# The last 64 outputs of a second matrix product, regrouped: two feed-forward blocks side by side instead of two halves of the tokens

## The chip, the cores and the metric

One core of one Trainium2 chip runs the kernel. The metric is device time in microseconds (us) of one execution, median of three runs. The product runs on TensorE (PE in the rows), the elementwise work on VectorE (DVE) and ScalarE (ACT); SyncE (SP) issues the DMAs. PE has two clock levels, 1.2 and 2.4 GHz; a granted clock of 1.00 is 2.4 GHz.

## The reference

```python
w = softmax(weight_gen, axis=-1)                     # (8, 4096, 8 heads, 7 taps)
x = sum over k of w[..., k] * x_pad[s + k]           # causal convolution, 8 heads of 24 channels
x = x.reshape(32768, 192)
h = x @ w_in                                         # 192 -> 2048
g = np.maximum(h, 0.0) ** 2
out = g @ w_out                                      # 2048 -> 192
```

All inputs and outputs are 32-bit floats.

## The kernel before

The 32768 tokens are worked in 64 chunks of 512. DVE does a chunk's softmax and convolution, the result goes through memory and back to be turned (tokens along the free dimension), and is then split into two 16-bit parts, `xh` on ACT and `xl` on DVE.

The first product (`mm1`, L560) makes the 2048 hidden values of a chunk in eight steps j of two blocks of 128. Three 16-bit products stand in for one 32-bit one, so a step has nine accumulation rounds of 512 columns. Every matmul uses a 64x64 quarter of the array, and four of them run side by side. ACT takes the relu (L567), the square (L571) and a 16-bit copy `gh` (L575); DVE makes the rest `gl` (L579).

The second product (`mm2_turned`, L608 and L612) serves chunks 4 to 62, 59 of them. It has 192 outputs, of which 128 go to the accumulator `acc0`, as two column halves of 64. The last 64 go to `acc1`: one column half of the array takes tokens 0 to 255 of the chunk, the other tokens 256 to 511, with the same weights. The two row halves of the array hold the two halves of a block's 128 hidden values; they write two different halves of the accumulator's free dimension, which have to be added at the end. `n` counts the three 16-bit products, `gh`, `gh` and `gl`.

The order of the work is written out by hand in one loop over chunks `c` and stages `b` = 0 to 3; each engine runs its own part of it in that order. A stage is two steps of `mm1`, then the second product of the stage before it. In stage (c, 1), ahead of the first `mm2` of chunk c, `finish` empties the accumulators of chunk c-1: ACT copies one half out (L674), DVE adds the other (L675). `store_turned` then scales (L697), turns 32x32 blocks (L698) and issues 24 DMAs on SP (L705). All this stands behind the two `low` (L579) of stage (c, 0) in DVE's order. Work of the convolution for later chunks is handed to stages by `plan_conv`, into the table `todo`, which runs at the end of a stage. Odd chunks also load the next group of two chunks at b = 0 (L109, L110), sum its magnitudes on ACT at b = 2 (L137), and make its scales at b = 3 in six short DVE instructions (L141 to L166, L151).

Of the kernel before, what the change touches and what calls it, by code (L numbers as in the profile page):

```python
# [8 lines left out]
F32 = mybir.dt.float32  # L9
# [4 lines left out]
ALU = mybir.AluOpType  # L14
# [14 lines left out]
def kernel(  # L29
# [9 lines left out]
    nc = tc.nc  # L39
    B, S, D = x.shape  # L40
# [3 lines left out]
    P = 128  # L44
# [4 lines left out]
    TC = 4  # L49
    NCH = n_chunks or R // TC  # L50
# [3 lines left out]
    D1 = 64  # L54
    ND = D // D1
    N = TC * P
    NJ = NF // 2
# [3 lines left out]
    N_PE = 3  # L61
# [8 lines left out]
    op = ctx.enter_context(tc.tile_pool(name="op", bufs=2))  # L70
# [13 lines left out]
    V = const.tile([P, NF, 3 * D], F16, name="V")  # L84
# [6 lines left out]
    act, ts, tt = nc.scalar.activation, nc.vector.tensor_scalar, nc.vector.tensor_tensor  # L91
# [100 lines left out]
    def block(j, i):  # L192
        return 4 * (j // 2) + 2 * i + j % 2
# [101 lines left out]
    HALVES = slice(0, D1), slice(D1, P)  # L295
# [240 lines left out]
    phs, rgs, ghs, gls, accs = {}, {}, {}, {}, {}  # L536

    def turned(c):
        return TURNED <= c < NCH - 1
# [33 lines left out]
    def high(c, j):  # L573
        gh = ghs[c, j] = gp.tile([P, 2, N], F16, name="gh")
        act(gh, rgs[c, j], AF.Copy, scale=1.0 / LIFT)  # L575
# [21 lines left out]
    def mm2_turned(c, j):  # L597
        if j == 0:
            new_accs(c)
        gh, gl = ghs.pop((c, j)), gls.pop((c, j))  # L600
        for i in range(2):
            fb = block(j, i)
            for n, g in enumerate((gh, gh, gl)):
                fl = dict(start=fb == 0 and n == 0, stop=fb == NF - 1 and n == 2)
                for col in HALVES:
                    for r, rows in enumerate(HALVES):
                        d = n * D + col.start
                        nc.tensor.matmul(accs[c][0][col, r], V[rows, fb, d:d + D1], g[rows, i], **fl)  # L608
                for m, col in enumerate(HALVES):
                    for r, rows in enumerate(HALVES):  # L610
                        d = n * D + P
                        nc.tensor.matmul(  # L612
                            accs[c][1][col, r, 0:N // 2], V[rows, fb, d:d + D1],
                            g[rows, i, m * N // 2:(m + 1) * N // 2], **fl,
                        )

    ends = {}

# [40 lines left out]
    outs, sums_t = {}, {}  # L659

    def finish(c, p):
        if c == 0:
            if p == 0:
                outs[c] = op.tile([P, TC, D], F32, name="o_sb")
            nc.scalar.copy(outs[c][:, 2 * p:2 * p + 2], accs[c][0][:, :, p * D:(p + 1) * D])
            return
        acc = accs[c][p]
        if turned(c):
            if p == 0:
                sums_t[c] = op.tile([P, TC * D], F32, name="s", bufs=1)  # L670
            n0, n1 = ((0, N), (N, N + N // 2))[p]
            n = n1 - n0
            tmp = op.tile([P, N], F32, name="tmp")
            nc.scalar.copy(tmp[:, 0:n], acc[:, 1, 0:n])  # L674
            tt(out=sums_t[c][:, n0:n1], in0=acc[:, 0, 0:n], in1=tmp[:, 0:n], op=ALU.add)  # L675
            return
        if p == 0:
            outs[c] = op.tile([P, TC, D], F32, name="o_sb")
        o = outs[c][:, 2 * p:2 * p + 2]
        f = falls[c // CPG]  # L680
        o = o.rearrange("p t d -> p (t d)")
        tmp = op.tile([P, N], F32, name="tmp")
        n = 2 * D
        act(tmp[:, 0:n], acc[:, 1, 0:n], AF.Copy, scale=f)
        stt(out=o, in0=acc[:, 0, 0:n], scalar=f, in1=tmp[:, 0:n], op0=ALU.mult, op1=ALU.add)  # L685

    def finish_last(c):
        o = outs[c]
# [4 lines left out]
    def store_turned(c):  # L693
        o = op.tile([P, TC * D], F32, name="o_sb")
        sm = sums_t.pop(c)
        sb = sm.rearrange("p (t n) -> p t n", n=P)
        tt(out=sb, in0=sb, in1=spread_falls[c // CPG].broadcast_to(sb.shape), op=ALU.mult)  # L697
        nc.vector.transpose(o, sm)  # L698
        for col in range(0, D, Q):
            for t in range(TC):  # L700
                if col < P:
                    p0, n0 = col, t * P
                else:
                    p0, n0 = 2 * t // TC * D1 + col - P, N + t % 2 * P
                nc.sync.dma_start(  # L705
                    out=out_v[:, c * TC + t, col:col + Q].rearrange("(q i) j -> i q j", i=Q),
                    in_=o[p0:p0 + Q, n0:n0 + P].rearrange("i (q j) -> i q j", j=Q),
                )

    def store(c):  # L710
        nc.sync.dma_start(out=out_v[:, c * TC:(c + 1) * TC, :], in_=outs[c])
# [128 lines left out]
    def at(c, b, f):  # L840
        todo.setdefault((c + b // NB, b % NB), []).append(f)
# [9 lines left out]
    def plan_conv(m):  # L851
        a, splits[m] = conv_steps(m, int(m < N_PE))
        if m == N_PE:
            for f in a[:6]:
                at(m - 2, 3, f)
            rows = splits.pop(m)
            for i, f in enumerate(a[6:-1]):
                at(m - 1, int(i > 4), f)
            between[m - 1, 1] = [a[-1], rows[0]]
            behind[m - 1, 1] = rows[1:]  # L860
            return
        for f in a[:3]:
            at(m - 2, 2 * int(m == N_PE + 1), f)
        if m > N_PE:
            spread(a[3:], m - 2, 1, pace.get(m, (0.25, 0.55, 0.73, 1)))

    pace = {N_PE + 1: (0, 0, 0.41, 0.7, 1), N_PE + 2: (0, 0.42, 0.72, 1)}
    splits = {}
    for u in range(1, NU):
        at(1, u - 1, cvt[NU + u][0])  # L870
        at(1, u, cvt[NU + u][1])
# [11 lines left out]
    for c in range(1, NCH + 1):  # L883
        for b in range(NB if c < NCH else 2):
            js = (2 * b, 2 * b + 1)
            if c < NCH:
                if b == 0 and c % 2 and (c + 3) // 2 * CPG < NCH:
                    load_group((c + 3) // 2)
                if c % 2 and b == 2 and (c + 3) // 2 * CPG < NCH:
                    total, scales = size_steps((c + 3) // 2)  # L890
                    b1 = 5 if c == 1 else 2
                    at(c, b1, total)
                    b2 = 6 if c == 1 else 3
                    at(c, b2, scales)
                    at(c, b2, lambda gi=(c + 3) // 2: descale(gi))
                if b == 0 and c + 2 < NCH and c + 2 > 2:
                    plan_conv(c + 2)
                for j in js:
                    mm1(c, j)
            early = b == 1 and 2 <= c <= TURNED  # L900
            if early:
                for p in range(2):
                    finish(c - 1, p)
            run(late)
            late.clear()
            if c == NCH and b == 1:
                finish_last(c - 1)
            elif b == (0 if c == NCH else 1) and c > 1:
                for p in range(0 if early else 2):
                    finish(c - 1, p)  # L910
                if turned(c - 1):
                    store_turned(c - 1)
                elif c < NCH:
                    store(c - 1)
            turn = turns.pop(c + 1, None) if b == NB - 1 else None
            if b == NB - 1 and c + 1 in splits and turn is None:
                for f in splits.pop(c + 1):
                    f()
            if pend and turn is None:
                mm2(*pend.pop(0))  # L920
            elif pend:
                one = pend.pop(0)
                mm2(*one, slice(0, 3))
                turn[0]()
                mm2(*one, slice(3, 4))
                turn[1]()
                mm2(*one, slice(4, 8))
            if c < NCH:
                relu(c, js[0])
                square(c, js[0])  # L930
                relu(c, js[1])
                high(c, js[0])
                sp = splits.pop(c + 1) if turn is not None else []
                run(sp[:1])
                square(c, js[1])
                run(sp[1:3])
                high(c, js[1])
                pend.append((c, b))
                late += [lambda c=c, j=js[0]: low(c, j)] + between.pop((c, b), [])
                late += [lambda c=c, j=js[1]: low(c, j)] + behind.pop((c, b), [])  # L940
                fs = todo.pop((c, b), [])
                if sp:
                    run(fs[:2])
                    run(sp[3:4])
                    run(fs[2:4])
                    run(sp[4:])
                    run(fs[4:])
                else:
                    run(fs)
# [30 lines left out]
```

## Time and profile before

| | |
|---|---|
| median of 3 runs | 2035.33 us (2034.96 to 2036.3) |
| the profiled execution | 2034.99 us |
| its span, first to last instruction | 2032.9 us |
| PE busy | 2024.2 us (100%), 42124 matmuls |
| weight loads | 1467.5 us (72%) |
| DVE busy | 1861.3 us (92%) |
| ACT busy | 1746.0 us (86%) |
| granted clock of PE | 1.000 |

Times in the rows are us from the first instruction. "Busy" is the union of an engine's instructions; ends of matmuls are modelled, so starts are what to compare. A row of a timeline gives the start, the time from there to the end of the last of the merged instructions, the engine, the line, the operation, the tiles written and read, the shape and the count; in brackets stands how long the engine was idle before it and who released it. Instructions of one engine overlap a little, so the start of the next one tells what one costs.

### The profile page before, as it was taken

The page shows a single profiled execution, that of the slowest core. Times are in us where ns is not written, and L with a number is a line of the kernel's source. Part 1 is how long each engine was busy: PE and PEld are TensorE (multiplying, and loading weights), DVE is VectorE, ACT ScalarE, POOL GpSimd, SP SyncE. Part 2 cuts the span into 40 slices and gives each one's busy share as a digit, 9 for nine tenths or more (in the row PEclk, how much of TensorE's full clock was granted, in tenths as well). Part 3 has the DMA queues.
Part 4 walks back from the last instruction along what each step waited for, and adds up shares of the span by engine and source line. Part 5 has one row for each costly group of instructions (what it writes and reads, how often), then busy time and mean ns, then how long its engine had stood idle before and what let it go on. Part 6 is the DMA issues. An engine that isn't in the chain of part 4 may idle for free.

```text
span 2032.9 us, 92331 instructions
## 1 busy us (share of the span) xinstructions
PE 2024.2 (100%) x42124; PEld 1467.5 (72%) x42124; DVE 1861.3 (92%) x2457; ACT 1746.0 (86%) x2011; POOL 5.4 (0%) x9
## 2 busy tenths in 40 slices
PE   9999999999999999999999999999999999999999
PEld 7777777777777777777777777777777777777776
DVE  8999999999999999999999999999999999999984
ACT  6888888888888888888888888888888888888887
POOL 1000000000000000000000000000000000000000
PEclk9999999999999999999999999999999999999999
DMA  6233333333332333233323333333233233333221
GB/s 189 67 95 86 79 65 76 89 94 76 69 84 74 96 83 83 62 79 89 93 73 64 91 75 94 84 76 70 73 95 93 72 65 82 82 95 78 59 60 23
DMA packets 303552, 164.02 MB, mean 81 GB/s; under 512 B 215360, under 2 KB 273728, under 8 KB 299192
## 3 DMA queue, kind: packets, MB, share of 16 engines
q1 hardware_dynamic: 303160, 158.11, 31.8%
q8 instruction: 329, 5.39, 1.1%
q14 instruction: 63, 0.52, 0.1%
HBM read 108.43 MB, written 49.56 MB: 78 GB/s over the span
## 4 chain that ended last, share of the span: by engine, by line
PE 95%; DVE 3%; DMA 1%; ACT 0%; SPq 0%; issue 0%; POOL 0%; DVEq 0%; POOLq 0%
PE ph L560 47%; PE acc L608 30%; PE acc L612 15%; PE acc L653 1%; PE acc L592 1%; DVE pr L339 1%; DVE pr L344 1%; DVE gl L579 1%; DMA xT<-xd 0%; DMA xl<-xd 0%; DMA xd<-xr 0%; DVE o_sb L685 0%; PE ph L628 0%; SPq L117 0%; DMA xt<-in_x_dram 0%
## 5 line engine op out<-in xcount | busy, mean ns | idle before, releaser
L560 PEld LDWEIGHTS <-W 64*64 64x64 f16 (+1 forms) x17568 | 633.7, 107 | 320.6 <-issue 4.1
L560 PE MATMUL ph<-xh,W 64*64 64x512 f16 (+1 forms) x11712 | 752.9, 376 | 0.0
L567 ACT ACTIVATE g<-ph 128x1024 f32<-128x1024 f32 x504 | 511.5, 1015 | 240.5 <-PE ph L560 240.5
L579 DVE SCALAR_TENSOR_TENSOR gl<-gh,g 128x1024 f16<-128x1024 f16 x504 | 609.2, 1220 | 110.5 <-ACT gh L575 99.7
L608 PE MATMUL acc<-gh,V 64*64 64x512 f16 x7552 | 696.3, 376 | 0.0
L612 PE MATMUL acc<-gh,V 64*64 64x256 f16 x7552 | 576.9, 269 | 0.1
L608 PEld LDWEIGHTS <-V 64*64 64x64 f16 x11328 | 406.7, 107 | 205.9 <-issue 1.3
L571 ACT ACTIVATE g<-g 128x1024 f32<-128x1024 f32 x512 | 538.7, 1052 | 8.0
L575 ACT ACTIVATE gh<-g 128x1024 f16<-128x1024 f32 x504 | 530.2, 1052 | 8.0
L560 PE MATMUL ph<-xl,W 64*64 64x512 f16 (+1 forms) x5856 | 427.0, 376 | 2.1 <-DMA xl<-xd 1.7
L612 PEld LDWEIGHTS <-V 64*64 64x64 f16 x11328 | 406.6, 107 | 17.3 <-issue 0.4
L339 DVE TENSOR_TENSOR pr<-xt,wt 128x768 f32<-128x768 f32 x434 | 408.2, 953 | 2.1
L608 PE MATMUL acc<-gl,V 64*64 64x512 f16 x3776 | 389.4, 376 | 0.5 <-DVE gl L579 0.5
L344 DVE TENSOR_TENSOR pr<-pr 128x768 f32<-128x768 f32 x376 | 358.4, 953 | 2.2
L612 PE MATMUL acc<-gl,V 64*64 64x256 f16 x3776 | 288.4, 269 | 0.0
L393 DVE TENSOR_TENSOR xl<-xT,xh 128x512 f16<-128x512 f32 x180 | 113.5, 686 | 21.5 <-ACT xh L387 20.8
L387 ACT CAST xh<-xT 128x512 f16<-128x512 f32 x180 | 98.5, 610 | 1.1 <-DMA xT<-xd 1.1
L653 PE MATMUL acc<-V,gh 64*128 64x192 f16 x960 | 62.1, 243 | 0.0
L520 DVE STREAM_TRANSPOSE xr<-pr 128x768 f32<-128x768 f32 x60 | 58.7, 978 | 2.1
L653 PE MATMUL acc<-V,gl 64*128 64x192 f16 x480 | 60.2, 243 | 0.1
L675 DVE TENSOR_TENSOR s<-acc,tmp 128x512 f32<-128x512 f32 x118 | 59.9, 549 | 0.0
L698 DVE STREAM_TRANSPOSE o_sb<-s 128x768 f32<-128x768 f32 x59 | 57.7, 978 | 2.1
(98 smaller groups left out, 661.7 us busy)
## 6 DMA issues: line engine op xcount, KB each, us to landing
xT<-xd SPq DMA_DIRECT2D x120, 384.0 KB
xt<-in_x_dram SPq DMA_DIRECT2D x31, 1344.0 KB
xd<-xr SPq DMA_DIRECT2D x240, 96.0 KB
out_dram<-o_sb SPq DMA_DIRECT2D x1416, 16.0 KB
wt<-in_weight_gen_dram SPq DMA_DIRECT2D x31, 224.0 KB
raw<-in_moe_w_in_dram SPq DMA_DIRECT2D x8, 384.0 KB
raw<-in_moe_w_out_dram SPq DMA_DIRECT2D x4, 768.0 KB
fd<-ft SPq DMA_DIRECT2D x124, 0.1 KB
```

Of the source, the lines that this page charges most:

```text
L339: tt(out=dst, in0=src, in1=taps_w[0][:, :, k:k + 1].broadcast_to([P, n, G]), op=ALU.mult)
L344: on.tensor_tensor(out=prs[k0], in0=prs[k0], in1=prs.pop(k), op=ALU.add)
L387: nc.scalar.copy(xh, xs)
L393: tt(out=xl, in0=xs, in1=xh, op=ALU.subtract)
L560: nc.tensor.matmul(to, w[rows, k, j % 2, col], xs, **fl)
L567: act(r, phs.pop((c, j)), AF.Relu, scale=RHO * LIFT ** 0.5)
L571: act(r, r, AF.Square)
L575: act(gh, rgs[c, j], AF.Copy, scale=1.0 / LIFT)
L579: stt(out=gl, in0=ghs[c, j], scalar=-LIFT, in1=rgs.pop((c, j)), op0=ALU.mult, op1=ALU.add)
L608: nc.tensor.matmul(accs[c][0][col, r], V[rows, fb, d:d + D1], g[rows, i], **fl)
L612: nc.tensor.matmul(accs[c][1][col, r, 0:N // 2], V[rows, fb, d:d + D1], g[rows, i, m * N // 2:(m + 1) * N // 2], **fl,)
L653: nc.tensor.matmul(accs[c][t // 2][:, h, t % 2 * D:(t % 2 + 1) * D], g[rows, i, t * P:(t + 1) * P], V[rows, fb, n * D:(n + 1) * D], start= ...
```

## The change

In the second product both blocks of a step now run in the same round n: first `acc0` for block 0 and block 1, then `acc1` with column half 0 of the array on block 0 and column half 1 on block 1, each over all 512 tokens. The two column halves of `acc1` now hold partial sums over different blocks, so `finish` takes all 512 columns of `acc1` too, into a tile `tmp`, and two new steps add the halves: `swap_thirds` copies each half to the other 64 partitions on ACT, and `add_thirds` adds on DVE. The store goes behind `add_thirds`, one stage later. The exponential of the softmax (L323), for chunks 5 on, runs behind the copies out of the accumulators.

```diff
-        for i in range(2):
-            fb = block(j, i)
-            for n, g in enumerate((gh, gh, gl)):
+        fbs = [block(j, i) for i in range(2)]
+        for n, g in enumerate((gh, gh, gl)):
+            for i, fb in enumerate(fbs):
                 fl = dict(start=fb == 0 and n == 0, stop=fb == NF - 1 and n == 2)
                 for col in HALVES:
                     for r, rows in enumerate(HALVES):
                         d = n * D + col.start
                         nc.tensor.matmul(accs[c][0][col, r], V[rows, fb, d:d + D1], g[rows, i], **fl)
-                for m, col in enumerate(HALVES):
-                    for r, rows in enumerate(HALVES):
-                        d = n * D + P
-                        nc.tensor.matmul(
-                            accs[c][1][col, r, 0:N // 2], V[rows, fb, d:d + D1],
-                            g[rows, i, m * N // 2:(m + 1) * N // 2], **fl,
-                        )
+            fl = dict(start=j == 0 and n == 0, stop=j == NJ - 1 and n == 2)
+            for i, col in enumerate(HALVES):
+                for r, rows in enumerate(HALVES):
+                    d = n * D + P
+                    nc.tensor.matmul(accs[c][1][col, r], V[rows, fbs[i], d:d + D1], g[rows, i], **fl)
...
+            tmp = op.tile([P, N], F32, name="tmp")
+            nc.scalar.copy(tmp, acc[:, 1])
             if p == 0:
-                sums_t[c] = op.tile([P, TC * D], F32, name="s", bufs=1)
-            n0, n1 = ((0, N), (N, N + N // 2))[p]
-            n = n1 - n0
-            tmp = op.tile([P, N], F32, name="tmp")
-            nc.scalar.copy(tmp[:, 0:n], acc[:, 1, 0:n])
-            tt(out=sums_t[c][:, n0:n1], in0=acc[:, 0, 0:n], in1=tmp[:, 0:n], op=ALU.add)
+                to = sums_t[c] = op.tile([P, TC * D], F32, name="s", bufs=1)
+            else:
+                to = thirds[c] = tmp
+            tt(out=to[:, 0:N], in0=acc[:, 0], in1=tmp, op=ALU.add)
...
+    def swap_thirds(c):
+        sw = thirds[c, "other"] = op.tile([P, N // 2], F32, name="sw", bufs=1)
+        for m, rows in enumerate(HALVES):
+            nc.scalar.copy(sw[rows], thirds[c][HALVES[1 - m], m * N // 2:(m + 1) * N // 2])
+
+    def add_thirds(c):
+        t, sw = thirds.pop(c), thirds.pop((c, "other"))
+        for m, rows in enumerate(HALVES):
+            tt(out=sums_t[c][rows, N:], in0=t[rows, m * N // 2:(m + 1) * N // 2], in1=sw[rows], op=ALU.add)
...
-                if turned(c - 1):
-                    store_turned(c - 1)
-                elif c < NCH:
+                if c < NCH and not turned(c - 1):
                     store(c - 1)
+            if b == 1 and c in exps:
+                exps.pop(c)()
+            if b == 2 and c < NCH and turned(c - 1):
+                add_thirds(c - 1)
+                store_turned(c - 1)
...
                 high(c, js[0])
+                if b == 1 and turned(c - 1):
+                    swap_thirds(c - 1)
```

How it moves instructions on DVE, around stages (c, 1) and (c, 2) of an odd chunk. `gl` is `low`, `acc` and `s` belong to `finish`, `s<-s,fs` and `o_sb<-s` to `store_turned`, `sm`, `wt` and `pr` to the convolution of a later chunk. Before:

```order
L579 SCALAR_TENSOR_TENSOR gl<-gh,g 128x1024 x2
L675 TENSOR_TENSOR s<-acc_21078,tmp 128x512
L675 TENSOR_TENSOR s<-acc_21079,tmp 128x256
L697 TENSOR_TENSOR s<-s,fs 128x768
L698 STREAM_TRANSPOSE o_sb<-s 128x768
L324 TENSOR_REDUCE sm<-wt 128x32
L325 TENSOR_SCALAR sm<-sm 128x32
L325 RECIPROCAL sm<-sm 128x32
L318 SCALAR_TENSOR_TENSOR wt<-wt,up,sm 128x224
L339 TENSOR_TENSOR pr<-xt,wt 128x768
L579 SCALAR_TENSOR_TENSOR gl<-gh,g 128x1024 x2
L339 TENSOR_TENSOR pr<-xt,wt 128x768 x2
```

Of the change:

```order
L579 SCALAR_TENSOR_TENSOR gl<-gh,g 128x1024 x2
L673 TENSOR_TENSOR s<-acc_19044,tmp 128x512
L673 TENSOR_TENSOR tmp<-acc_19045,tmp 128x512
L324 TENSOR_REDUCE sm<-wt 128x32
L325 TENSOR_SCALAR sm<-sm 128x32
L325 RECIPROCAL sm<-sm 128x32
L318 SCALAR_TENSOR_TENSOR wt<-wt,up,sm 128x224
L339 TENSOR_TENSOR pr<-xt,wt 128x768
L579 SCALAR_TENSOR_TENSOR gl<-gh,g 128x1024 x2
L695 TENSOR_TENSOR s<-tmp,sw 64x256 x2
L707 TENSOR_TENSOR s<-s,fs 128x768
L708 STREAM_TRANSPOSE o_sb<-s 128x768
L339 TENSOR_TENSOR pr<-xt,wt 128x768 x2
```

The scaling and the turning went from ahead of the two `gl` of stage (c, 1) to behind them, and two half adds went in front of them.

On ACT, in stage (c, 1), `sw` is what `swap_thirds` writes and `wt<-wt` is the exponential. Of the change:

```order
L668 COPY tmp<-acc_17564 128x512
L668 COPY tmp<-acc_17565 128x512
L323 ACTIVATE wt<-wt 128x224
L567 ACTIVATE g<-ph 128x1024
L571 ACTIVATE g<-g 128x1024
L567 ACTIVATE g<-ph 128x1024
L575 ACTIVATE gh<-g 128x1024
L690 COPY sw<-tmp 64x256 x2
L571 ACTIVATE g<-g 128x1024
L575 ACTIVATE gh<-g 128x1024
```

Before, the exponential stood ahead of the two copies, the second copy had 256 columns, and nothing stood between the first `gh` (L575) and the second square (L571).

## Rows read from the trace of the kernel before

**Rows 1.** Part 4 of the page: the chain that ended last, by line.

```profile
PE ph L560 47%; PE acc L608 30%; PE acc L612 15%; PE acc L653 1%; PE acc L592 1%; DVE pr L339 1%; DVE pr L344 1%; DVE gl L579 1%; DMA xT<-xd 0%; DMA xl<-xd 0%; DMA xd<-xr 0%; DVE o_sb L685 0%; PE ph L628 0%; SPq L117 0%; DMA xt<-in_x_dram 0%
```

**Rows 2.** Waits of PE alone: total us, times, longest; the one from chunk 4 on.

```profile
PE acc L608 <- DVE gl L579: 0.5, 1, 0.5
```

**Rows 3.** Timeline of PE, one stage of two steps, and the start of the next.

```profile
997.44 1.49 PE L560 MATMUL ph<-xh,W 64*64 64x512 f16 x24
...
1001.32 0.41 PE L608 MATMUL acc<-gh,V 64*64 64x512 f16 x4
...
1005.22 1.49 PE L560 MATMUL ph<-xh,W 64*64 64x512 f16 x24
```

**Rows 4.** Timeline of DVE, stage (c, 1) of an odd chunk.

```profile
1006.81 1.01 DVE L675 TENSOR_TENSOR s<-acc,tmp 128x512 f32<-128x512 f32 x2
1007.85 0.96 DVE L697 TENSOR_TENSOR s<-s,fs 128x768 f32<-128x768 f32 x1
...
1009.75 0.34 DVE L324 TENSOR_REDUCE sm<-wt 128x32 f32<-128x224 f32 x1
...
1013.44 1.22 DVE L579 SCALAR_TENSOR_TENSOR gl<-gh,g 128x1024 f16<-128x1024 f16 x1
1014.58 0.95 DVE L339 TENSOR_TENSOR pr<-xt,wt 128x768 f32<-128x768 f32 x1
```

**Rows 5.** Timeline of ACT, the same stage.

```profile
1011.27 1.05 ACT L571 ACTIVATE g<-g 128x1024 f32<-128x1024 f32 x1
1012.35 1.06 ACT L575 ACTIVATE gh<-g 128x1024 f16<-128x1024 f32 x1
```

**Rows 6.** Timeline of ACT: copies between partition halves at the start; short instructions of an even chunk.

```profile
17.60 1.50 ACT L378 COPY xT<-ph 64x256 f32<-64x256 f32 x4
...
1036.70 0.39 ACT L323 ACTIVATE wt<-wt 128x224 f32<-128x224 f32 x1
1037.00 0.84 ACT L674 COPY tmp<-acc 128x512 f32<-128x512 f32 x2
```

**Rows 7.** Groups of DVE by shape, 500 to 1000 us: busy, mean ns | idle.

```profile
L675 DVE TENSOR_TENSOR s<-acc,tmp 128x512 f32<-128x512 f32 x16 | 10.9, 684 | 0.0
L675 DVE TENSOR_TENSOR s<-acc,tmp 128x256 f32<-128x256 f32 x16 | 6.6, 416 | 0.0
```

**Rows 8.** Timeline of DVE: two half-height copies at the start; three full-height in a row.

```profile
15.97 1.42 DVE L376 COPY xT<-acc 64x512 f32<-64x512 f32 x2
...
1023.20 1.90 DVE L393 TENSOR_TENSOR xl<-xT,xh 128x512 f16<-128x512 f32 x3 [0.75 <-ACT xh L387]
```

**Rows 9.** Busy times between 1014.58 and 1036.59: PE, PEld, DVE, ACT, POOL; clock, DMA.

```profile
1014.58:1036.59 22.01, 22.01 (x485) 15.95 (x481) 19.83 (x29) 20.55 (x23) 0.00 (x0) 1.00 0.12 19
```

**Rows 10.** Timeline of DVE, stage (c, 1) of the even chunk that follows.

```profile
1036.59 2.35 DVE L579 SCALAR_TENSOR_TENSOR gl<-gh,g 128x1024 f16<-128x1024 f16 x2
1038.86 1.01 DVE L675 TENSOR_TENSOR s<-acc,tmp 128x512 f32<-128x512 f32 x2
```

**Rows 11.** Timeline of PE: first second product of the odd and of the even chunk.

```profile
1009.11 0.41 PE L608 MATMUL acc<-gh,V 64*64 64x512 f16 x4
...
1040.25 0.41 PE L608 MATMUL acc<-gh,V 64*64 64x512 f16 x4
```

**Rows 12.** Timeline of SP: loads, stores of an odd chunk, stores at the end.

```profile
994.87 0.43 SPq L110 DMA_DIRECT2D xt<-in_x_dram  x1
...
1009.85 14.32 SPq L705 DMA_DIRECT2D out_dram<-o_sb  x24
...
2006.42 13.66 SPq L705 DMA_DIRECT2D out_dram<-o_sb  x24
2028.58 2.08 SPq L691 DMA_DIRECT2D out_dram<-o_sb  x4
```

**Rows 13.** Timeline of ACT: the first use of the group loaded at 994.87.

```profile
1021.10 1.47 ACT L137 ACTIVATE junk<-xt 128x1536 bf16<-128x1536 f32 x1
```

**Rows 14.** Busy times from 124 to 130 us, columns as in rows 9.

```profile
124.00:130.00 6.00, 4.93 (x83) 3.80 (x84) 6.00 (x7) 4.05 (x5) 0.00 (x0) 1.00 0.74 244
```

More of the change, by code (lines that the diff above doesn't have):

```diff
@@ L685, in finish @@
         stt(out=o, in0=acc[:, 0, 0:n], scalar=f, in1=tmp[:, 0:n], op0=ALU.mult, op1=ALU.add)
+    thirds = {}
+    def swap_thirds(c):
[6 more added lines that the diff above has]
+            tt(out=sums_t[c][rows, N:], in0=t[rows, m * N // 2:(m + 1) * N // 2], in1=sw[rows], op=ALU.add)
     def finish_last(c):
@@ L861, in plan_conv @@
             return
-        for f in a[:3]:
-            at(m - 2, 2 * int(m == N_PE + 1), f)
+        if m == N_PE + 1:
+            for f in a[:3]:
+                at(m - 2, 2, f)
+        else:
+            for f in a[:2]:
+                at(m - 2, 0, f)
+            exps[m - 2] = a[2]
         if m > N_PE:
@@ L867 @@
     pace = {N_PE + 1: (0, 0, 0.41, 0.7, 1), N_PE + 2: (0, 0.42, 0.72, 1)}
-    splits = {}
+    splits, exps = {}, {}
     for u in range(1, NU):
```

## The prediction, made before the changed kernel ran

> **What bounds the kernel now.** I read the chain that ended last first: nearly all of it is PE, the first product 47%, the second 30% and 15% [rows 1]. Then PE's waits: from chunk 4 on there is one, of 0.5 us, for a `gl` [rows 2]. So in steady state PE never waits, and a chunk takes what its matmuls take: from the first second product of one chunk to that of the next, 1009.11 to 1040.25, it is 31.14 us [rows 11]. Third, the timelines of DVE and ACT around the place where the accumulators are emptied: there one reads how much time is left before PE needs them. That slack is what this change spends.
>
> **What PE gains.** A stage of `mm1` takes 997.44 to 1001.32, 3.88 us for 18 rounds of four matmuls of 512 columns, 0.2156 us each; a stage of `mm2` takes 1001.32 to 1005.22, 3.90 us for 12 pairs of a 512- and a 256-column round [rows 3]. At 2.4 GHz, the granted level, 12 pairs of 768 columns are 3.84 us, so 24 rounds carry 0.06 us beyond their columns, 2.5 ns each. The change leaves the columns as they are (2 x 512 + 2 x 256 = 3 x 512 for each n) and makes nine rounds of twelve in a step. That saves 3 x 2.5 ns per step, 0.06 us per chunk, and 3.5 us over 59 chunks. The halved weight traffic of the last outputs gains nothing more: the 256-column rounds run at their columns already. The single wait for `gl` [rows 2] should go, -0.5 us, since `gl` is now used in the last third of a step and no longer in the middle.
>
> **What is added and moved, odd chunk.** DVE empties the accumulators, then scales and turns (1007.85 to 1009.75, 1.90 us), does the softmax, and reaches the second `gl` of the stage at 1013.44, just as ACT's second `gh` ends (1012.35 + 1.06) [rows 4, 5]. Now:
>
> - `swap_thirds` goes in front of the square at 1011.27 [rows 5], and delays that `gh` and so the `gl`. Its two 64x256 copies between halves: four such in a row took 1.50 us, 0.375 each [rows 6]. With the 0.1 us of overlap lost where the partitions change, 0.88. From below: 0.60, if they follow each other like the 224-column exponential and its successor (0.30) [rows 6]; from above 1.0, if each is as long as the exponential was with its 0.39, and the gaps grow.
> - DVE's 1.90 us of scaling and turning leave the place ahead of that `gl`. There they were free, and they gain nothing now: DVE waits for ACT instead. They return behind it.
> - The two half adds follow the `gl`. A 256-column add lasts 0.416 [rows 7]. Full-height instructions of 512 columns follow each other at 0.60 (three in 1.90), half-height ones that change halves at 0.71 (two in 1.42) [rows 8]: the second does not overlap. So 2 x 0.445 = 0.89; 0.75 if they did overlap.
> - The add of `acc1` goes from 256 to 512 columns: +0.27 [rows 7].
> - The exponential behind the copies gains nothing. In the even chunk the copies end at 1037.84 [rows 6], and the add begins at 1038.86, behind the two `gl` [rows 10]. Nor does it cost: its reader, the reduction, now comes right behind the adds, and the exponential's 0.39 us are over by then.
>
> On the overlap, the Trainium skill speaks against this change too. "VectorE: DVE Perf Modes", section "Two Vector instructions with no wait between them", says in effect that an instruction which starts in another group of 32 partitions than its predecessor is held until everything before it has finished. The 0.71 against 0.60 of rows 8 agrees; by the rule the half adds are 0.89, without it 0.75, some 4 us of the whole.
>
> So DVE passes 1014.58 [rows 4] late by 0.88 + 0.89 + 1.90 = **3.67 us**. From there to 1036.59, the `gl` of the even chunk, it was idle for 22.01 - 19.83 = 2.18 us [rows 9]. (0.3 of that are gaps between dependent instructions, which stay; as much comes back as overlap where a wait vanishes.) So the lag at the even chunk's adds is 3.67 - 2.18 = **1.49 us**.
>
> **What is late then.** Before, those adds end at 1038.86 + 0.68 = 1039.54 and at 1039.87 [rows 7, 10]; PE needs the accumulators at 1040.25 [rows 11]. Slack 0.70 and 0.37. Now the first add ends at 1041.03. PE arrives 0.06 earlier, at 1040.19; with 0.05 for the signal it waits **0.90 us**. The second ends at 1039.87 + 1.49 + 0.27 = 1041.63; `acc1` is needed two rounds after the start, at 1041.52, another **0.16**. Nothing else on DVE comes too late: `xl` of the odd chunk was done at 1025.10 and waited 0.75 [rows 8], so it is late by under 3.67 - 0.75 = 2.9; the next chunk's `mm1` begins three stages of 7.78 after 1005.22 [rows 3], at 1028.6, 3.5 us later, and reads `xl` in the seventh of nine rounds. The stall of 1.06 us comes once in two chunks. From the even to the odd chunk the same 3.5 us of lag meet more idle time (no six short instructions for the scales, no sum on ACT), PE itself is a microsecond later, and the odd chunk's adds end at 1007.82 for a need at 1009.11 [rows 4, 11], a slack of 1.3. Even chunks behind an odd one that makes scales are 6 to 60, **28 of them**.
>
> **Sum.** Per pair 1.06 - 2 x 0.06 = 0.94; 28 x 0.94 = 26.3; three chunks more, -0.2; the `gl` wait, -0.5; stores at the end, +0.2 (below): **+25.8 us**. The profiled execution took 2034.99, so 2060.8; the median of three runs, 2035.33, stands 0.3 higher: **2061 us**. With the costs from below (0.60 and 0.75) the lag is 1.07, the stall 0.64, the sum +14: 2049. From above (1.0 and 0.96, 0.1 more for the signal) 2068.
>
> **Stores and loads.** SP issues a chunk's 24 stores in 14.3 us [rows 12]. They start a stage later, near 1018, end near 1033, and push an odd chunk's load from 994.87 to about 1002 [rows 12]. ACT first needs it at 1021.10 [rows 13]. Covered; if not, ACT and then PE wait. At the end the stores of chunk 62 began at 2006.42; now about 2015, so they end near 2028.9 where the last four start at 2028.58 [rows 12]: 0.2 us.
>
> **Rivals.**
> *No stall.* The point of decision is the lag at the even chunk's adds: below about 0.4 us PE never waits, and only the matmuls' 3.5 and the 0.5 us remain, 2031.3. For it: two of the three parts of the 3.67 are measured on instructions of other shapes or places. Against: even with both at nothing the 1.90 would have to vanish in 2.18 of idle time, and neither can cost nothing.
> *A small stall,* 0.3 to 0.6 us, because the copies are cheaper than the nearest row: 2036 to 2048.
> *Late loads or a DVE that never catches up.* DVE has 8% of 31.14 us to spare, 2.4, and gets 1.16 per chunk, so it stays short of bound; but if the odd chunks stall by as little as 0.3 us as well, or the load takes over 19 us, the time is 2070 or more.
> *A large fixed cost per matmul.* If a round's fixed part were ten times the 2.5 ns that I take from rows 3, because a part of it hides in the columns' time, 24 rounds less in a chunk would save 0.6 us, 35 us in all, and with 28 stalls of 1.06 us it came to some 2029. Against it: 512- and 256-column rounds together leave no room for more than 2.5 [rows 3]. The Trainium skill, "TensorEngine Tiling (Array Packing)", section "Instruction Overhead", states about 60 cycles of overhead for each matmul, an estimated 25 ns at 2.4 GHz; here the trace disagrees.
> A lower clock is none: from 124 to 130 us PE was idle for 1.07 us and the granted clock stayed at 1.00 [rows 14].
>
> **How the numbers follow.** A measurement of this kernel tells about 0.2%, 4 us, from no change. Stall as worked out, 2048 to 2068: 0.66. Small stall: 0.12 (0.03 of it within 4 us). No stall: 0.14, and since its 4.1 us lie on that bound, half to either side. Large fixed cost: 0.02. Worse: 0.06. Faster 0.07 + 0.02 = 0.09; the same 0.07 + 0.03 = 0.10; slower 0.81. The likeliest case's own range is 2048 to 2068; for 8 in 10 the small stall is needed as well, so 2036 to 2069.
>
> **What would show it.** Right: in the waits of PE a line L608 on DVE's add (L673), 28 times, some 0.9 us each, with L613 on the same add behind it at 0.1 to 0.2; the time between the first second products 31.08 us into odd chunks and 32.1 into even ones; DVE idle for 1 to 2 us ahead of the second `gl` of stage (c, 1), and the two `sw` copies at 0.375 each. Wrong: no such line (then the lag was absorbed, and the starts of the adds show where), or PE waiting for `xl` or for a DMA.

## The result and the profile after

The changed kernel takes **2059.88 us** (median of four, 2059.75 to 2060.07) against 2035.19; the ratio is 1.012, 95% interval 1.0108 to 1.0133. The forecast was 2061 in a range of 2036 to 2069. The profiled execution took 2060.07 us with a span of 2058.3, so by its own time the change costs 25.1 us; between the medians it is 24.7.

PE, which waited for nothing in steady state before [rows 2], now waits for DVE. The waits of PE alone from 165 us on (total us, times, longest):

```profile
PE acc L608 <- DVE s L673: 19.3, 28, 1.0
```

L673 is the add that empties an accumulator; it comes 28 times, as often as an even chunk follows an odd one that makes scales. The matmuls in front of a wait end late in the model, so the starts tell more. The timeline of PE at the first second product of an odd chunk, of the even chunk behind it, and of the next odd one:

```profile
1020.09 0.63 PE L608 MATMUL acc<-gh,V 64*64 64x512 f16 x8
...
1050.52 0.84 PE L560 MATMUL ph<-xl,W 64*64 64x512 f16 x12
1052.03 0.63 PE L608 MATMUL acc<-gh,V 64*64 64x512 f16 x8 [0.67 <-DVE s L673]
1052.63 0.41 PE L613 MATMUL acc<-gh,V 64*64 64x512 f16 x4
...
1083.28 0.63 PE L608 MATMUL acc<-gh,V 64*64 64x512 f16 x8
```

The two steps are 31.94 and 31.25 us, where they were 31.14 each [rows 11]. The rounds alone would be 31.08 (the kernels without stalls, below), so the even chunk starts 0.86 late. In it `acc1` (L613) begins 0.60 behind `acc0`, where without a wait it begins 0.43 behind (1020.09 to 1020.52 in the odd chunk); the other 0.17 are lost there. Together a stall of 1.03 us per pair.

Where DVE's time goes, in the odd chunk and at the adds of the even one (timeline of DVE):

```profile
1022.39 1.22 DVE L579 SCALAR_TENSOR_TENSOR gl<-gh,g 128x1024 f16<-128x1024 f16 x1 [0.69 <-ACT gh L575]
1025.41 1.22 DVE L579 SCALAR_TENSOR_TENSOR gl<-gh,g 128x1024 f16<-128x1024 f16 x1 [1.79 <-ACT gh L575]
1026.55 0.84 DVE L695 TENSOR_TENSOR s<-tmp,sw 64x256 f32<-64x256 f32 x2
1027.42 0.96 DVE L707 TENSOR_TENSOR s<-s,fs 128x768 f32<-128x768 f32 x1
1028.42 0.98 DVE L708 STREAM_TRANSPOSE o_sb<-s 128x768 f32<-128x768 f32 x1
1029.32 1.79 DVE L339 TENSOR_TENSOR pr<-xt,wt 128x768 f32<-128x768 f32 x2
...
1049.03 2.35 DVE L579 SCALAR_TENSOR_TENSOR gl<-gh,g 128x1024 f16<-128x1024 f16 x2
1051.30 0.68 DVE L673 TENSOR_TENSOR s<-acc,tmp 128x512 f32<-128x512 f32 x1
1051.90 0.68 DVE L673 TENSOR_TENSOR tmp<-acc,tmp 128x512 f32<-128x512 f32 x1
```

These answer to [rows 4, 10]. DVE idles 1.79 us in front of the second `gl` of the odd chunk, where scaling and turning stood before; then half adds, scaling and turning (1026.55 to 1029.32) run behind it. What follows runs with hardly a gap up to the `gl` of the even chunk (busy times of PE, PEld, DVE, ACT, POOL, as in [rows 9]):

```profile
1029.32:1049.02 19.70, 19.70 (x372) 13.16 (x365) 19.42 (x29) 18.57 (x22) 0.00 (x0) 1.00 0.16 26
```

Of 2.18 us of idle time 0.28 are left, the gaps between dependent instructions. The `acc0` add ends at 1051.98 and PE starts at 1052.03.

The timeline of ACT shows what holds the `gl` of 1025.41 back, the two copies between `gh` and the second square, against [rows 5]:

```profile
1020.41 1.01 ACT L567 ACTIVATE g<-ph 128x1024 f32<-128x1024 f32 x1
1021.32 1.04 ACT L575 ACTIVATE gh<-g 128x1024 f16<-128x1024 f32 x1
1022.39 0.82 ACT L690 COPY sw<-tmp 64x256 f32<-64x256 f32 x2
1023.23 1.06 ACT L571 ACTIVATE g<-g 128x1024 f32<-128x1024 f32 x1
1024.32 1.06 ACT L575 ACTIVATE gh<-g 128x1024 f16<-128x1024 f32 x1
```

The `gh` begins 0.91 behind the relu, which lasts 1.01: neighbours overlap by 0.10. Between the end of `gh` at 1022.36 and the square lie 0.87 us now, so with the lost overlap the square is 0.97 late.

### The profile page after: what moved, and what is told of

Its sections match the earlier page's. It is cut to its first block, busy times and chain, and to the rows that moved or that the text cites. A ratio compares the mean times of both kernels' runs of the same rounds, so it can differ in the third digit from the quotient of the medians.

```text
span 2058.3 us, 81094 instructions
## 1 busy us (share of the span) xinstructions
PE 2030.6 (99%) x36460; PEld 1356.7 (66%) x36460; DVE 1905.9 (93%) x2575; ACT 1813.6 (88%) x2129; POOL 5.4 (0%) x9
## 4 chain that ended last, share of the span: by engine, by line
PE 53%; DVE 31%; ACT 9%; SPq 3%; issue 2%; DMA 2%; DVEq 0%; POOL 0%; POOLq 0%
PE ph L560 25%; PE acc L608 16%; DVE gl L579 10%; PE acc L613 8%; DVE pr L344 6%; DVE pr L339 5%; ACT g L571 3%; ACT gh L575 3%; ACT g L567 3%; SPq L715 2%; PE acc L651 2%; DVE xl L393 2%; DVE xr L520 1%; DVE o_sb L708 1%; DVE s L707 1%
## 5 line engine op out<-in xcount | busy, mean ns | idle before, releaser
L560 PEld LDWEIGHTS <-W 64*64 64x64 f16 (+1 forms) x17568 | 640.4, 107 | 339.1 <-issue 4.7
L579 DVE SCALAR_TENSOR_TENSOR gl<-gh,g 128x1024 f16<-128x1024 f16 x504 | 598.6, 1218 | 111.7 <-ACT gh L575 111.2
L608 PE MATMUL acc<-gh,V 64*64 64x512 f16 x7552 | 592.8, 376 | 19.3 <-DVE s L673 19.3
L608 PEld LDWEIGHTS <-V 64*64 64x64 f16 x11328 | 404.1, 107 | 229.5 <-issue 28.2
L571 ACT ACTIVATE g<-g 128x1024 f32<-128x1024 f32 x512 | 539.3, 1054 | 9.4
L575 ACT ACTIVATE gh<-g 128x1024 f16<-128x1024 f32 x504 | 530.1, 1052 | 8.0
L613 PE MATMUL acc<-gh,V 64*64 64x512 f16 x3776 | 389.1, 377 | 0.0
L608 PE MATMUL acc<-gl,V 64*64 64x512 f16 x3776 | 296.5, 376 | 0.0
L613 PEld LDWEIGHTS <-V 64*64 64x64 f16 x5664 | 204.8, 107 | 110.6 <-issue 7.8
L613 PE MATMUL acc<-gl,V 64*64 64x512 f16 x1888 | 194.6, 376 | 0.0
L668 ACT COPY tmp<-acc 128x512 f32<-128x512 f32 x118 | 62.3, 580 | 0.0
```

The costliest lines, as they stand in the source:

```text
L560: nc.tensor.matmul(to, w[rows, k, j % 2, col], xs, **fl)
L571: act(r, r, AF.Square)
L579: stt(out=gl, in0=ghs[c, j], scalar=-LIFT, in1=rgs.pop((c, j)), op0=ALU.mult, op1=ALU.add)
L613: nc.tensor.matmul(accs[c][1][col, r], V[rows, fbs[i], d:d + D1], g[rows, i], **fl)
```

## The experiments

Two theories. *Place*: the added work and the moved store stand on the one stretch of DVE, from the odd chunk's second `gl` to the even chunk's adds, whose 2.18 us of idle time they overrun. *Load*: DVE has 1.15 us more per chunk, and where it stands does not matter. Beside them, that the new order of matmuls is slower in itself.

### The regrouped matmuls alone

The kernel before, with `mm2_turned` of the change and nothing else.

> The regrouped matmuls in the kernel before, and nothing else; the second column half of the last 64 outputs is left out of the sum, so no copies between halves, no half adds, and the store stays where it was. Theory (the loss comes from what DVE and ACT have to do around the accumulators): PE gains 3.5 us from the rounds saved and 0.5 us from the one wait for gl, 2031.2 us (2030.7 to 2031.8), and PE waits for nothing from chunk 4 on. Rival (the new order of matmuls is itself slower on PE): 2035 or more. Rival (a large fixed cost per round goes): 2000.

2031.25 us; ratio 0.9979, interval 0.9970 to 0.9988. From 165 us on no wait of PE is listed. Twelve rounds per step became nine, and the timeline of PE shows the second step of a stage at 1001.68, 1.94 us behind the first:

```profile
999.74 0.63 PE L608 MATMUL acc<-gh,V 64*64 64x512 f16 x8
...
1001.68 0.63 PE L608 MATMUL acc<-gh,V 64*64 64x512 f16 x8
```

Before, a stage of two steps took 3.90 [rows 3], 1.95 each. PE's part of the change is a gain of the forecast size. Neither the slower order nor a large fixed cost per round holds.

### The copies between halves out of the way

```diff
                 high(c, js[0])
-                if b == 1 and turned(c - 1):
-                    swap_thirds(c - 1)
...
                 high(c, js[1])
+                if b == 1 and turned(c - 1):
+                    swap_thirds(c - 1)
```

> The change, with the two copies between partition halves behind the second gh of the stage instead of in front of the second square. Theory (place): the second gl of the odd chunk comes 0.97 us earlier, the lag at the even chunk's adds falls by as much, the first add ends 0.1 us ahead of PE's need, and only the wait for acc1, about 0.1 us in 28 chunks, is left: 2033 us (2031 to 2036). Rival (load: DVE has 1.15 us more per chunk than before, wherever it stands): DVE's instructions are the same, so 2060.

2032.78 us; ratio 0.9987, interval 0.9977 to 0.9996. The same instructions on every engine, and 27 us less than the change. The timelines of DVE and PE at an even chunk:

```profile
975.82 0.68 DVE L673 TENSOR_TENSOR s<-acc,tmp 128x512 f32<-128x512 f32 x1
976.42 0.68 DVE L673 TENSOR_TENSOR tmp<-acc,tmp 128x512 f32<-128x512 f32 x1
```

```profile
976.63 0.63 PE L608 MATMUL acc<-gh,V 64*64 64x512 f16 x8
977.15 0.41 PE L613 MATMUL acc<-gh,V 64*64 64x512 f16 x4
```

The first add ends at 976.50, 0.13 ahead of PE. The second ends at 977.10, and L613 begins 0.52 behind L608 where 0.43 is free of waiting: 0.09 us in 28 chunks, 2.5 us, are left. Load falls with this run.

### The store in two parts

```diff
-                add_thirds(c - 1)
-                store_turned(c - 1)
+                add_thirds(c - 1)
+                store_part(c - 1, 1)
...
+                if turned(c - 1):
+                    store_part(c - 1, 0)
```

`store_part` is `store_turned` on columns 0 to 511 and 16 stores (part 0, behind the adds), or on columns 512 to 767 and 8 stores (part 1).

> The change, with the scaling, the turning and the stores of the first 128 outputs back in stage (c, 1), behind the adds; only those of the last 64 wait for the half adds in stage (c, 2). The copies stay where the change has them. Theory (place): the 1.90 us behind the second gl shrink to about 0.8, the lag by 1.1 us, and no wait of PE is left: 2031.5 us (2031 to 2034). Rival (load): DVE has two instructions more and no less to do, so 2060 or more.

2030.72 us; ratio 0.9977, interval 0.9968 to 0.9986. DVE has two instructions more per chunk, and from 165 us on no wait of PE is listed. Timeline of DVE, odd chunk:

```profile
943.73 0.68 DVE L711 TENSOR_TENSOR s<-s,fs 128x512 f32<-128x512 f32 x1
944.44 0.71 DVE L712 STREAM_TRANSPOSE o_sb<-s 128x512 f32<-128x512 f32 x1
...
949.92 1.23 DVE L579 SCALAR_TENSOR_TENSOR gl<-gh,g 128x1024 f16<-128x1024 f16 x1 [1.27 <-ACT gh L575]
951.06 0.84 DVE L695 TENSOR_TENSOR s<-tmp,sw 64x256 f32<-64x256 f32 x2
951.94 0.43 DVE L711 TENSOR_TENSOR s<-s,fs 128x256 f32<-128x256 f32 x1
952.40 0.45 DVE L712 STREAM_TRANSPOSE o_sb<-s 128x256 f32<-128x256 f32 x1
952.77 0.92 DVE L339 TENSOR_TENSOR pr<-xt,wt 128x768 f32<-128x768 f32 x1
```

The part in front of the `gl` fills time in which DVE waited for ACT; behind it stand 0.83 us (951.94 to the next product at 952.77) in place of 1.90. The slack is thin: at an even chunk the `acc0` add ends at 975.44 and PE starts at 975.68, 0.24 us. By the starts of PE's rounds two even chunks still lose time at the adds, 0.07 us in chunk 10 and 0.31 in chunk 20; ahead of chunk 20 DVE had stood still once for 0.22 us (at 654.13), for nothing that the profile shows.

### The copies twice

```diff
-        for m, rows in enumerate(HALVES):
+        for m, rows in [*enumerate(HALVES)] * 2:
```

> The change, with the two copies between partition halves done twice over. Theory (place): nothing absorbs them, the second gl of the odd chunk comes 0.83 us later (two copies of 0.403 with their gaps), and so do the even chunk's adds: 28 x 0.83 = 23 us more, 2083 us (2079 to 2087). Rival (load): DVE's work is unchanged and ACT has 1 us and more to spare in that stage, 2060 to 2062.

2084.26 us; ratio 1.0241, interval 1.0227 to 1.0256: 24.4 us above the change. The waits of PE from 165 us on:

```profile
PE acc L608 <- DVE s L673: 42.8, 28, 1.9
```

Against 19.3 that is 23.5 us more in the same 28 waits, 0.84 each. The timeline of ACT at one of them:

```profile
968.07 1.05 ACT L575 ACTIVATE gh<-g 128x1024 f16<-128x1024 f32 x1
969.13 1.68 ACT L690 COPY sw<-tmp 64x256 f32<-64x256 f32 x4
970.83 1.06 ACT L571 ACTIVATE g<-g 128x1024 f32<-128x1024 f32 x1
```

From the first `gh` to the square it is 2.76 us, where the change takes 1.91 (1021.32 to 1023.23): the added pair of copies costs 0.85. What is put on the stretch now goes into the time one to one. With the two runs before it the cause is shown from both sides.

### The moves alone

The kernel before, with the store one stage later and the exponential behind the copies.

> The kernel before, with only the two moves of the change: the store one stage later, the exponential behind the copies. No regrouping, no copies between halves, no half adds. Theory (place): DVE passes the second gl of the odd chunk late by the 1.90 us of scaling and turning alone, less than the 2.18 us that it was idle from there to the next adds; the adds are about in time and the time is that of before, 2035.3 us (2034.8 to 2036.5). Rival (the move of the store is the loss by itself): 28 stalls, 2045 or more.

2033.83 us; ratio 0.9991, interval 0.9982 to 1.0. The 1.90 us alone are absorbed: the two moves together are no loss, and from chunk 5 on every chunk takes 31.14 us as before. The time is 1.5 us below that of before, and below the range of the theory, which said the same time. 1.0 of it lies in chunk 4: from its first second product to that of chunk 5 it is 31.14 us (167.01 to 198.15) where the kernel before takes 32.15 (below). Another 0.3 lies ahead of chunk 4's first second product (167.01 and 167.32); what is then left between the medians is in no part of the two profiles.

### The exponential back in its place

```diff
-            for f in a[:2]:
+            for f in a[:3]:
                 at(m - 2, 0, f)
-            exps[m - 2] = a[2]
```

> The change, with the exponential back where it was, ahead of the copies out of the accumulators. Prediction's claim (its place neither gains nor costs, since the adds wait for the two gl on DVE and not for the copies): 2059.9 us (2059 to 2061). Rival (the copies ahead of it bring the adds forward): more, 28 x 0.3 = 8 us, 2068.

2060.45 us; ratio 1.0123, interval 1.0110 to 1.0137; 0.6 above the change. In steady state its place does nothing: the waits for L673 sum to 19.1 us. Of the 0.4 us between the two profiled spans 0.36 lie in chunk 4 (below).

### The half adds in the other order

```diff
-        for m, rows in enumerate(HALVES):
+        for m, rows in ((1, HALVES[1]), (0, HALVES[0])):
```

> The change, with the two half adds in the other order, partitions 64 to 127 first. Now the first of them changes halves against the gl ahead of it, too. If an instruction that changes halves waits until everything before it has ended, each stall grows by the overlap of 0.08 us that is lost there and by about 0.03 of gap: 28 x 0.1 = 2.5 us more, 2062.4 us (2061.8 to 2063). If the change of halves costs nothing: 2059.9.

2063.14 us; ratio 1.0137, interval 1.0123 to 1.0151: 3.3 us above the change, 0.12 per stall, just over the range. Timeline of DVE:

```profile
963.12 1.23 DVE L579 SCALAR_TENSOR_TENSOR gl<-gh,g 128x1024 f16<-128x1024 f16 x1 [1.79 <-ACT gh L575]
964.38 0.85 DVE L695 TENSOR_TENSOR s<-tmp,sw 64x256 f32<-64x256 f32 x2
965.27 0.96 DVE L707 TENSOR_TENSOR s<-s,fs 128x768 f32<-128x768 f32 x1
```

From `gl` to the first half add there are now 1.26 us, 0.03 more than the `gl` lasts; in the change it was 1.14, an overlap of 0.08. Here the half add that begins in the other half of the partitions starts behind the end of its predecessor. The rule of the Trainium skill that the prediction cited ("VectorE: DVE Perf Modes", section "Two Vector instructions with no wait between them") says so, and this run agrees with it, 0.12 us an instance. The scaling (L707) no longer changes halves against the add in front of it, yet starts no sooner, 0.04 us behind it; that it waits for what the adds wrote, as L697 does behind L675 in the kernel before (0.03) [rows 4], is the likely reason and is not shown.

### Both repairs

The copies late, the store in two.

> The copies between halves behind the second gh, and the store split in two as well. Theory (place): the lag at the even chunk's adds is 2 us less than in the change, PE never waits, and the time is the floor that the regrouped matmuls set, that of the matmuls alone, 2031 us (2030.3 to 2031.6); no gain over the split store alone, since no wait is left there either.

**2029.88 us**; ratio 0.9973, interval 0.9962 to 0.9984; 0.4 us below the range. From chunk 5's first second product to chunk 62's it takes 1771.56 us, as the matmuls alone do; chunk 4 takes 31.08 and not 31.44 (below), and the rest of the difference to that run lies ahead of chunk 4 (166.83 and 167.99). This and the store in two alone are the fastest versions here, 0.2 to 0.3% below the kernel before. The timelines of DVE and PE at an even chunk:

```profile
973.55 0.68 DVE L673 TENSOR_TENSOR s<-acc,tmp 128x512 f32<-128x512 f32 x1
974.15 0.68 DVE L673 TENSOR_TENSOR tmp<-acc,tmp 128x512 f32<-128x512 f32 x1
```

```profile
974.91 0.60 PE L608 MATMUL acc<-gh,V 64*64 64x512 f16 x8
975.34 0.39 PE L613 MATMUL acc<-gh,V 64*64 64x512 f16 x4
```

The add ends 0.68 us ahead of PE, as it did in the kernel before (0.70), and both chunks of a pair take 31.08 us. The store in two alone had 0.24 us of slack and lost 0.38 us in two chunks; here no chunk is longer than 31.08. So the second repair adds slack and hardly speed. Of the 0.6 us between their profiled spans, 0.4 are those two chunks, 0.4 lie ahead of chunk 4's first second product (167.22 and 166.83), where the code is the same, and the end gives 0.1 back.

## Why the prediction was right, point by point

- **PE's gain.** Forecast 0.06 us a chunk, 3.5 in all. The run of the matmuls alone is 4.3 us below the kernel before, 0.7 of it in chunk 4, and its chunks take 31.08 for 31.14. The 60 cycles a matmul of the Trainium skill ("TensorEngine Tiling (Array Packing)", section "Instruction Overhead") show in no round here.
- **The copies.** Forecast 0.88 (0.60 to 1.0). Measured 0.97: they last 0.403 each, for 0.375 of the row taken [rows 6], and overlap with nothing. The term was 0.09 short, inside its bounds. (The parts that the prediction names for it, twice 0.375 and 0.1, make 0.85 and not 0.88.)
- **The half adds.** Forecast 0.89; from 1026.55 to 1027.42 they take 0.87.
- **Scaling and turning.** Forecast 1.90; 1027.42 to 1029.32 is 1.90. That they gave nothing in their old place shows in the 1.79 us of idle time there.
- **Absorbed.** Forecast 2.18; measured 2.30. The same 29 instructions of DVE took 22.01 us before [rows 9] and take 19.71 now (1029.32 to 1049.03): the idle time fell from 2.18 to 0.28, and 0.41 of busy time came back as overlap. The forecast let the gaps that stay and the overlap that returns cancel at 0.3.
- **The lag.** Forecast 1.49. The even chunk's adds begin 31.21 us behind the odd chunk's first second product (1020.09 to 1051.30) and began 29.75 behind it [rows 10, 11]: 1.46. That it fits within 0.03 is partly luck, since the copies and the absorbed time were both forecast about 0.1 too low, and the one adds what the other takes away.
- **The stall.** Forecast 0.90 for `acc0` and 0.16 for `acc1`; measured 0.86 and 0.17. The 0.05 for the signal, for which the prediction names no row, is what 1051.98 to 1052.03 shows. 28 times was right, and so was the other parity: odd chunks start on time.
- **Stores and loads.** No wait of PE for a transfer came up in steady state. At the end, the time behind chunk 62's first second product is 0.4 us longer, for 0.2 forecast. The timeline of SP, against [rows 12]: the stores were all issued before the last four, but those four took 2.55 us to issue and not 2.08. Why is open.

```profile
2040.20 12.76 SPq L715 DMA_DIRECT2D out_dram<-o_sb  x24
2053.52 2.55 SPq L701 DMA_DIRECT2D out_dram<-o_sb  x4
```

The step that failed is small: "The exponential behind the copies gains nothing", and with it the 0.5 us for the one `gl` wait, which was put down to the later use of `gl` alone. The claim was read in a steady even chunk and holds there. In stage (4, 1), where chunk 3 is emptied, it does not. The timeline of ACT there, of the kernel before:

```profile
165.76 0.39 ACT L323 ACTIVATE wt<-wt 128x224 f32<-128x224 f32 x1 [2.18 <-DVE wt L322]
166.06 1.03 ACT L684 ACTIVATE tmp<-acc,f 128x384 f32<-128x384 f32 x2
```

and of the change:

```profile
163.70 1.04 ACT L682 ACTIVATE tmp<-acc,f 128x384 f32<-128x384 f32 x2
165.98 0.39 ACT L323 ACTIVATE wt<-wt 128x224 f32<-128x224 f32 x1 [1.25 <-DVE wt L322]
```

ACT waited 2.18 us for the softmax on DVE, with the copies out of the accumulators queued behind the exponential. DVE waited for those copies in turn, and its `gl` came late. The timelines of DVE and PE, of the kernel before:

```profile
166.65 1.14 DVE L685 SCALAR_TENSOR_TENSOR o_sb<-acc,f,tmp 128x384 f32<-128x384 f32 x2 [0.93 <-ACT tmp L684]
167.71 2.35 DVE L579 SCALAR_TENSOR_TENSOR gl<-gh,g 128x1024 f16<-128x1024 f16 x2
```

```profile
167.32 0.41 PE L608 MATMUL acc<-gh,V 64*64 64x512 f16 x4
167.85 0.30 PE L612 MATMUL acc<-gh,V 64*64 64x256 f16 x4
...
168.17 0.30 PE L612 MATMUL acc<-gh,V 64*64 64x256 f16 x4
168.98 0.41 PE L608 MATMUL acc<-gl,V 64*64 64x512 f16 x4 [0.50 <-DVE gl L579]
```

By the starts PE lost twice here: `acc1` begins 0.53 behind `acc0` and not 0.22, and the round of `gl` 0.81 behind L612 and not 0.11. That is 1.01 us, of which the list of waits has 0.5.

From the first second product of chunk 4 to that of chunk 5 the kernel before takes 32.15 us (167.32 to 199.47), the change 31.08 (167.49 to 198.57), the change with the exponential back in place 31.44 (167.69 to 199.13). Of the 1.07 us the rounds are 0.06. The other 1.01 has two cures that overlap. The moves alone take all of it: 31.14, as in every later chunk. The regrouped matmuls with the exponential in its old place use `gl` later and take 0.65, whether alone (31.44 too) or in the change, and leave 0.36. So the exponential's place is worth 0.36 us beside the regrouping and 1.01 without it, and not nothing.

The sum: from chunk 5's first second product to chunk 62's the change takes 198.57 to 1999.45, 1800.88 us, and the kernel before 199.47 to 1974.44, 1774.97. That is 25.9 more; with the 57 x 0.06 that the rounds give back it makes 29.3, or 1.05 for each of 28 stalls, forecast at 1.06. (27 of them take 1.01 to 1.05; the one at chunk 54 takes 0.34 more, and why is open.) Chunk 4 gives 1.07 back, start and end take 0.6: 25.4 us of span, 25.1 of time (24.7 between the medians), for a forecast of 25.8.

## What to carry to other kernels

Slack belongs to a place. An engine that is busy 92% of the time took 1.15 us more per chunk at no cost once it stood where the engine waited anyhow, and the same work cost 1.2% where it stood between a late start and a deadline. So before a step is moved behind a wait, walk the engine's queue from that wait to the next point at which another engine needs it, sum what is added, and subtract only the idle time inside that stretch; and when a step is added to two engines in turn, put the first part behind what the second engine is waiting for.

## What the runs showed of the hardware that was not expected

ACT, too, seems to lose its overlap where the partitions change: the copies between halves leave gaps of 0.01 to 0.03 us around them, where `gh` and the square otherwise overlap by 0.1. And four 64-column weight loads for each round were no bound even for the 256-column rounds: halving the rounds of `acc1` took the load time from 72% to 67% of the span in the run of the matmuls alone, and gave 2.5 ns per saved round (0.06 us a chunk for 24 rounds), no more.
